# Sigmoid attention followed by a gated feed-forward layer: group 0's keys taken by key tiles, one query load and one sigmoid moved

## The chip, the cores and the metric

The kernel runs on one core of one Trainium2 chip. The metric is the device time of one execution in microseconds; lower is better. Of several timed runs the median counts. Beside the timed runs one execution was profiled, and every view below is of that execution.

The engines are called as in the profile: PE is the matrix engine (PEld its weight loads), DVE the vector engine, ACT the scalar engine, POOL and SP two engines that do little here but issue transfers. POOL's transfers convert fp32 in memory to fp16 on chip; SP's don't convert.

## The reference

Inputs are `q`, `k`, `v` of shape (8, 12, 448, 64), `w_in` (768, 2048), `w_out` (2048, 768) and `beta` (2048). The output has 8 x 448 = 3584 rows of 768.

```python
scores = q @ k.T / sqrt(64) - log(448)          # per batch and head, 448 x 448
attn   = 1 / (1 + exp(-scores))                 # a sigmoid, no sum over keys
x      = (attn @ v), heads side by side         # (3584, 768)
h      = x @ w_in
g      = h * 1 / (1 + exp(-beta * h))
out    = g @ w_out
```

## The kernel before

**Groups.** A group is four heads of one batch, laid on 128 partitions as four strips of 32, so a batch has three groups (0, 1, 2) and there are 24 in all. A strip's 32 partitions hold 14 consecutive rows each; in the code a partition's 14 rows are its "blocks" `c`. The 448 keys are worked in four key tiles: three of 128 and a last one of 64. Key tile j takes, of every partition, the rows j, j + 3, j + 6 and j + 9; the last tile takes rows 12 and 13. So the columns that belong to one key tile lie in four pieces in a partition's row.

**One group's way.** `load_one` (L110) brings a group's queries or keys as fp16 into `raw`. `transpose` turns them on DVE: queries by L191, the first three key tiles in one instruction by L199, the last by L203. Scores are matmuls of the transposed keys and queries (L213) into PSUM tiles `sco`, each of two banks. ACT turns a whole `sco` tile into attention weights (L224). `attend` multiplies them with the values (L279), and DVE copies the result as fp16 to `xT` (L288). `load_v` (L131, L138) loads a batch's values.

**The layer behind it.** `dense1` is one unit of work: six matmuls (L166) of `xT` with 128 columns of `w_in` into one PSUM bank, a sigmoid on ACT with `beta` as scale (L305), and a product on DVE (L308) into `gt`. `dense2` and, for most rows, a seven-product scheme multiply `gt` with `w_out`; stores go out from SP. There are four single PSUM banks for these units and the attention results, handed out in turn; a unit waits for the DVE instruction that last read its bank.

**Order.** All instructions are ordered by hand. The units stand in one list, and `fill_units(n)` emits the next n of them between pieces of attention. Batch 0 is special: it is done in two halves of 224 queries. `half_visit(g, c0, second)` makes the scores of half a group, for key tiles 0 and 1 (`second` = 0) or 2 and 3, and `attend` follows. The first halves of all three groups come first, with a few idle matmuls between them (L533), then the second half of group 0, then `dense1` units 0 to 15 for the first half (unit `dc` uses columns 128 dc on), between which stand the second halves of groups 1 and 2. From batch 1 on, `visit(g, jt)` makes the scores of all queries and one key tile, and a planner with fixed costs (`M1H_US` and others) decides how many units follow each visit. A visit emits its score matmuls, then two attention sigmoids, then the units.

**Loads at the start.** Group 0's first query half and all its keys come as fp32 through SP's queue (L517) into memory that `gt` uses later. DVE and ACT cast them to fp16: queries on DVE (L537), the first half of each partition's key columns on DVE (L540), the second half on ACT (L539). Everything else comes through POOL's queue, in this order: queries' first half and keys of groups 1 and 2, values of batch 0, the second query halves of groups 0, 1 and 2, then `w_in` in eight chunks of 256 columns (`load_w_in`, L148), so that chunk c feeds units 2c and 2c + 1, then group 3, `w_out` (L156) and the values of batch 1. POOL's queue works in order. The program gives its transfers eight semaphores in turn, and a transfer waits for the landing of the eighth before it.

Of the kernel before, what the change touches and what calls it, by code (L numbers as in the profile page):

```python
# [8 lines left out]
FP32 = mybir.dt.float32  # L9
FP16 = mybir.dt.float16  # L10
# [3 lines left out]
def kernel(  # L14
# [10 lines left out]
    nc = tc.nc  # L25
# [3 lines left out]
    B, H, S, D = q.shape  # L29
    NTOK, DM = out.shape  # L30
    DFF = moe_w_in.shape[1]
    P = 128
    BLK = 32
# [152 lines left out]
    def transpose(g: int, r: int, c0: int = 0, c1: int = NB):  # L186
        raw = raws[g][:, r]
        if r == 0:
            if g not in qT:
                qT[g] = qTp.tile([P, NB * BLK, PAIR], FP16, tag="qT", name="qT")  # L190
            nc.vector.transpose(  # L191
                out=in_order(g // QPB, qT[g][:, c0 * BLK : c1 * BLK]),
                in_=raw[:, c0:c1].rearrange("p c d -> p (c d)").bitcast(FP32),
            )
            return
        kT[g] = kTp.tile([P, S, PAIR], FP16, tag="kT", name="kT")
        to = kT[g].rearrange("p k e -> p (k e)").bitcast(FP32)
        frm = raw.rearrange("p c d -> p (c d)").bitcast(FP32).rearrange("p (c f) -> p c f", c=NB)
        nc.vector.transpose(  # L199
            out=to[:, 0 : JF * P].rearrange("p (j i q) -> p i j q", j=JF, i=HQ),  # L200
            in_=frm[:, 0:NF].rearrange("p (i j) f -> p i j f", j=JF),
        )
        nc.vector.transpose(  # L203
            out=to[:, JF * P :], in_=frm[:, NF:].rearrange("p c f -> p (c f)")
        )

    def score_tile():
# [23 lines left out]
        return at  # L231


    def visit(g: int, jt: int, also=()):
        if jt < JF:
            todo = [(score_tile(), [s]) for s in (2 * g, 2 * g + 1)]
        else:
            todo = [(score_tile(), [2 * h, 2 * h + 1]) for h in (g, *also)]
        for e in range(PAIR):
            for sco, slots in todo:  # L240
                for s in slots:
                    for hh in range(2):
                        score(sco, 0, s, jt, hh, e, 0, S)
        for sco, slots in todo:
            at = weigh(sco, S)
            for s in slots:
                at_tiles[s, jt, 0] = at
# [259 lines left out]
    with tc.manual_schedule():  # L507
        raws[0] = rawp.tile([P, 2, NB, D], FP16, tag="raw", name="raw")
        wide = gt.rearrange("p a b -> p (a b)").bitcast(FP32)
        cut = NH * D  # L510
        early = [(0, 0, NH), (1, 0, NB)]
        staged = {}
        at = 0
        for r, c0, c1 in early:
            staged[r] = wide[:, at : at + (c1 - c0) * D]
            at += (c1 - c0) * D
            nc.sync.dma_start(  # L517
                out=staged[r],
                in_=(q, k)[r][0, 0:HQ].rearrange("h (p c) d -> (h p) (c d)", c=NB)[
                    :, c0 * D : c1 * D  # L520
                ],
            )
        nc.gpsimd.memset(dummy, 0.0)  # L523
        nc.scalar.activation(out=dummy, in_=dummy, func=AF.Sigmoid, bias=0.0, scale=1.0)

# [7 lines left out]
                nc.tensor.matmul(idle, still[:, 0:P], still, start=True, stop=True)  # L533

        idle_units(9)
        raw = raws[0].rearrange("p r c d -> p r (c d)")
        nc.vector.tensor_copy(out=raw[:, 0, 0:cut], in_=staged[0])  # L537
        transpose(0, 0, 0, NH)
        nc.scalar.copy(out=raw[:, 1, cut:], in_=staged[1][:, cut:])  # L539
        nc.vector.tensor_copy(out=raw[:, 1, 0:cut], in_=staged[1][:, 0:cut])  # L540
        transpose(0, 1)
        for g in range(1, QPB):
            load_one(g, 0, 0, NH)
            load_one(g, 1)
        load_v(0)
        nc.sync.dma_start(out=beta_in[0:NDC], in_=moe_beta.rearrange("(c p) -> c p", p=P))
        for g in range(QPB):
            load_one(g, 0, NH, NB)
        for c in range(WCH):
            load_w_in(c)  # L550
        for g in range(1, QPB):
            transpose(g, 0, 0, NH)
# [10 lines left out]
        half_visit(0, QH, 0)  # L563
        attend(1, 0, QH)
        half_visit(0, QH, 1)
        for g in range(1, QPB):
            transpose(g, 0, NH, NB)
        attend(2, 0, QH, (0,))
        attend(2, 0, QH, (1,))
# [12 lines left out]
        firsts.close()  # L582
        share_psum(ctx, 2, 4)
        fill_units(4)
        for g in range(1, QPB):
            for second in range(2):
                half_visit(g, QH, second)
                if second:
                    attend(g - 1, QH, QH)
                fill_units(g if second else 2 + g)  # L590
        fill_units(1)
        attend(QPB - 1, QH, QH)
        fill_units(1)
        transpose(QPB, 0)
        transpose(QPB, 1)
# [24 lines left out]
        for i, (g, jt, also) in enumerate(visits):  # L620
            if jt == 0:
# [68 lines left out]
```

## Time and profile before

| what | value |
|---|---|
| timed runs | 383.72, 383.92, 384.61 us; median 383.92 |
| profiled execution | 383.76 us, of which the span of instructions is 382.0 |
| PE busy | 375.9 us, 98% of the span |
| DVE, ACT, POOL busy | 231.8, 229.5, 66.4 us |
| granted PE clock | 1.00 |
| transfers | 34.71 MB in 42405 packets |

The page cuts the span in 40 equal slices of 9.55 us and gives the busy share of each engine in tenths. The chain of waits follows the last instruction back to what released it, step by step. A timeline's row has the start, the length, the engine, the line, what is written and read, and in brackets the idle time just before and what ended it. Matmuls are pipelined and their ends are modelled, so a pause of PE is read more safely from starts than from ends. The GB/s of the transfer views count bytes written on chip; where POOL's queue converts, twice as many are read.

### The profile page before, as it was taken

How to read it: one execution, taken by the hardware profiler on the slowest of the kernel's cores; microseconds unless marked ns; L12 is line 12 of the kernel's file. 1: busy time of each engine (PE TensorE's matmuls, PEld its weight loads, DVE VectorE, ACT ScalarE, POOL GpSimd, SP SyncE). 2: the span in 40 equal slices, each digit the busy share in tenths (PEclk: the TensorE clock that was granted, in tenths of full speed). 3: DMA queues.
4: the chain of work that ended last, by engine and by line, in shares of the span. 5: the costliest groups of instructions: out<-in, count | busy, mean ns of one | idle time of the engine just before them, and what ended most of it. 6: DMA issues, size and time to landing. Idle time of an engine off the chain costs nothing.

```text
span 382.0 us, 8227 instructions
## 1 busy us (share of the span) xinstructions
PE 375.9 (98%) x3415; PEld 199.2 (52%) x3415; DVE 231.8 (61%) x439; ACT 229.5 (60%) x330; POOL 66.4 (17%) x114
## 2 busy tenths in 40 slices
PE   8999999999999999999999999999999999999996
PEld 3478754444654445444554445544456444555563
DVE  3447366775765557555775657665676665655761
ACT  5987856697465786487355782477752787435200
POOL 7833343140110410040110410113100000000000
PEclk9999999999999999999999999999999999999999
DMA  9999999845363930563363750649303300030033
GB/s 165 172 196 204 198 205 209 178 65 59 50 132 83 122 51 2 130 90 32 50 132 84 102 69 2 131 88 118 50 0 84 85 1 2 2 82 0 2 82 125
DMA packets 42405, 34.71 MB, mean 91 GB/s; under 512 B 21872, under 2 KB 38656, under 8 KB 42368
## 3 DMA queue, kind: packets, MB, share of 16 engines
q0 software_dynamic: 36688, 22.47, 43.5%
q1 hardware_dynamic: 5680, 11.71, 11.6%
q8 instruction: 27, 0.44, 0.5%
q14 instruction: 10, 0.08, 0.1%
HBM read 45.62 MB, written 11.01 MB: 148 GB/s over the span
## 4 chain that ended last, share of the span: by engine, by line
PE 92%; DMA 4%; POOL 1%; issue 1%; ACT 0%; DVE 0%; ACTq 0%; POOLq 0%
PE m_ps L166 73%; PE sco L213 10%; PE av_ps L279 9%; DMA w_in<-in_moe_w_in_dram 3%; DMA raw<-in_k_dram 2%; POOL raw L110 1%; POOL w_in L148 1%; ACT attnT L224 0%; ACT sg L305 0%; DVE osb L340 0%; DVE gt L308 0%; POOL dummy L523 0%; ACTq L305 0%; POOLq L674 0%
## 5 line engine op out<-in xcount | busy, mean ns | idle before, releaser
L224 ACT ACTIVATE attnT<-sco 128x896 f16<-128x896 f32 (+1 forms) x171 | 145.2, 902 | 81.1 <-PE sco L213 80.5
L166 PE MATMUL m_ps<-xT,w_in 128*128 128x448 f16 (+2 forms) x1014 | 154.7, 336 | 0.7 <-DMA w_in<-in_moe_w_in_dram 0.5
L308 DVE TENSOR_TENSOR gt<-m_ps,sg 128x448 f16<-128x448 f32 (+1 forms) x144 | 81.4, 572 | 81.6 <-ACT sg L305 78.1
L166 PEld LDWEIGHTS <-w_in 128*128 128x128 f16 (+1 forms) x1014 | 82.8, 101 | 69.3 <-issue 15.1
L305 ACT ACTIVATE sg<-m_ps,beta_sb 128x448 f32<-128x448 f32 (+1 forms) x144 | 84.3, 597 | 36.9 <-PE m_ps L166 29.8
L166 PEld LDWEIGHTS <-sum 128*64 128x64 f16 (+1 forms) x664 | 48.1, 104 | 33.5 <-issue 7.9
L213 PE MATMUL sco<-qT,kT 32*128 32x448 f16 (+3 forms) x864 | 52.0, 341 | 0.7 <-DVE kT L199 0.5
L166 PE MATMUL m_ps<-w_T,sum 128*128 128x384 f16 (+1 forms) x360 | 51.6, 327 | 0.0
L110 POOL DMA_DIRECT2D raw<-in_q_dram x26 | 14.4, 553 | 181.0 <-DVE kT L203 175.5
L428 DVE TENSOR_TENSOR osb<-m_ps,osb 128x384 f32<-128x384 f32 x60 | 33.3, 555 | 18.8 <-PE m_ps L166 16.9
L166 PEld LDWEIGHTS <-gt 128*128 128x128 f16 (+1 forms) x414 | 31.4, 103 | 23.8 <-issue 6.2
L279 PE MATMUL av_ps<-attnT,v 128*64 128x448 f16 (+3 forms) x432 | 40.2, 338 | 0.0
L398 DVE TENSOR_TENSOR sum<-gt 128x1024 f16<-128x1024 f16 x60 | 39.1, 677 | 0.1
L288 DVE CAST xT<-av_ps 128x448 f16<-128x448 f32 (+1 forms) x54 | 28.5, 567 | 15.3 <-PE av_ps L279 14.3
L166 PE MATMUL m_ps<-w_T,gt 128*64 128x384 f16 (+1 forms) x268 | 34.3, 327 | 0.0
L166 PE MATMUL m_ps<-w_out,sum 128*64 128x384 f16 (+1 forms) x304 | 33.8, 327 | 0.0
L279 PEld LDWEIGHTS <-v 128*64 128x64 f16 (+1 forms) x432 | 20.6, 108 | 18.8 <-issue 9.2
L213 PEld LDWEIGHTS <-kT 32*128 32x128 f16 (+1 forms) x864 | 13.7, 96 | 28.6 <-issue 25.7
L166 PE MATMUL m_ps<-w_out,gt 128*128 128x384 f16 (+3 forms) x146 | 22.6, 327 | 0.0
L131 POOL DMA_DIRECT2D v<-in_v_dram x32 | 19.8, 632 | 10.4 <-DMA w_in<-in_moe_w_in_dram 5.6
L191 DVE STREAM_TRANSPOSE qT<-raw 128x448 f32<-128x448 f32 (+1 forms) x27 | 16.6, 616 | 0.4 <-DMA raw<-in_q_dram 0.3
L431 ACT COPY osb<-m_ps 128x384 f32<-128x384 f32 x12 | 5.8, 481 | 16.8 <-PE m_ps L166 16.8
(25 smaller groups left out, 90.1 us busy)
## 6 DMA issues: line engine op xcount, KB each, us to landing
out_dram<-osb SPq DMA_DIRECT2D x98, 96.0 KB, 1.9
raw<-in_k_dram POOLq DMA_DIRECT2D x23, 224.0 KB, 5.3
raw<-in_q_dram POOLq DMA_DIRECT2D x21, 224.0 KB, 3.9
v<-in_v_dram POOLq DMA_DIRECT2D x32, 144.0 KB, 6.5
w_in<-in_moe_w_in_dram POOLq DMA_DIRECT2D x8, 384.0 KB, 10.7
w_out<-in_moe_w_out_dram POOLq DMA_DIRECT2D x4, 768.0 KB, 13.8
v<-in_v_dram POOLq DMA_DIRECT2D x16, 48.0 KB, 5.9
out_dram<-osb SPq DMA_DIRECT2D x2, 384.0 KB, 3.0
```

Source lines behind the costliest of these rows:

```text
L110: nc.gpsimd.dma_start(out=raws[g][:, r, c0:c1].rearrange("p c d -> p (c d)"), in_=(q, k)[r][b, HQ * t : HQ * (t + 1)].rearrange("h (p c) d ...
L131: nc.gpsimd.dma_start(out=vs[b][i * BLK : (i + 1) * BLK, :, 0:JF].rearrange("p h j d -> p h (j d)"), in_=rows[:, :, JF * i * D : JF * (i + ...
L166: nc.tensor.matmul(to[c : c + step], hidden[:, c : c + step], weights, **({} if step == P else {"tile_position": (0, c)}), **flags,)
L191: nc.vector.transpose(out=in_order(g // QPB, qT[g][:, c0 * BLK : c1 * BLK]), in_=raw[:, c0:c1].rearrange("p c d -> p (c d)").bitcast(FP32),)
L213: nc.tensor.matmul(sco[base : base + nk, hh, u0 : u0 + n], kT[g][lo : lo + BLK, jt * P : jt * P + nk, e], qT[g][lo : lo + BLK, c0 : c0 + n ...
L224: nc.scalar.activation(out=at[:, :, 0:n], in_=sco[:, :, 0:n], func=AF.Sigmoid, bias=NEG_LOG_S, scale=MSCALE,)
L279: nc.tensor.matmul(av[hh * D : (hh + 1) * D, 0:n], vs[b][base : base + nk, 2 * (s % NPAIR) + hh, jt], at[base : base + nk, hh, 0:n], start ...
L288: nc.vector.tensor_copy(out=xTs[b][:, s % NPAIR, c0 : c0 + n], in_=av[:, 0:n])
L305: nc.scalar.activation(out=sg[:, 0:n], in_=m1[:, 0:n], func=AF.Sigmoid, bias=0.0, scale=beta_sb[:, dc : dc + 1])
L308: nc.vector.tensor_tensor(out=gt[:, dc, off : off + n], in0=m1[:, 0:n], in1=sg[:, 0:n], op=ALU.mult)
L398: nc.vector.tensor_tensor(out=sums[t, i], in0=x, in1=y, op=op)
L428: nc.vector.tensor_tensor(out=out, in0=in0, in1=in1, op=op)
```

## The change

Three things are changed. PE's instructions stay the same in number and order.

1. Group 0's keys come in three transfers instead of one, cut by key tiles: tiles 0 and 1, tile 2, the last tile. The queries' transfer stays ahead of them. The runs of consecutive bytes are shorter: 512 runs of 512 bytes, 512 of 256, 128 of 512, where there were 128 of 3584. The casts are cut the same way: tile 0 on DVE, tile 1 on ACT, tile 2 and the last on DVE. A new function `transpose_keys(g, j0, j1)` transposes a range of key tiles, and for group 0 it is called for tiles 0 and 1, then (after the casts of the others) for tile 2 and for the last.
2. Group 2's second query half is loaded after four chunks of `w_in` instead of ahead of all eight, and its transpose moves from before `attend(2, 0, ...)` to before `attend(0, QH, QH)`. The loop over the second halves is written out; the units between them are the same.
3. In the third visit of batch 1 (index 2 of the list of visits) one `dense1` unit is emitted between the two attention sigmoids, and the planner counts it. On PE its place is the same; on ACT its sigmoid now stands between the two others.

```diff
-        kT[g] = kTp.tile([P, S, PAIR], FP16, tag="kT", name="kT")
+        transpose_keys(g, 0, JF)
+        transpose_keys(g, JF, JF + 1)
+
+    def transpose_keys(g: int, j0: int, j1: int):
+        if g not in kT:
+            kT[g] = kTp.tile([P, S, PAIR], FP16, tag="kT", name="kT")
         to = kT[g].rearrange("p k e -> p (k e)").bitcast(FP32)
-        frm = raw.rearrange("p c d -> p (c d)").bitcast(FP32).rearrange("p (c f) -> p c f", c=NB)
+        frm = raws[g][:, 1].rearrange("p c d -> p (c d)").bitcast(FP32)
+        frm = frm.rearrange("p (c f) -> p c f", c=NB)
+        if j0 == JF:
+            nc.vector.transpose(
+                out=to[:, JF * P :], in_=frm[:, NF:].rearrange("p c f -> p (c f)")
+            )
+            return
         nc.vector.transpose(
-            out=to[:, 0 : JF * P].rearrange("p (j i q) -> p i j q", j=JF, i=HQ),
-            in_=frm[:, 0:NF].rearrange("p (i j) f -> p i j f", j=JF),
-        )
-        nc.vector.transpose(
-            out=to[:, JF * P :], in_=frm[:, NF:].rearrange("p c f -> p (c f)")
+            out=to[:, j0 * P : j1 * P].rearrange("p (j i q) -> p i j q", i=HQ, q=BLK),
+            in_=frm[:, 0:NF].rearrange("p (i j) f -> p i j f", j=JF)[:, :, j0:j1],
         )
...
-    def visit(g: int, jt: int, also=()):
+    def visit(g: int, jt: int, also=(), between=None):
...
-        for sco, slots in todo:
+        for x, (sco, slots) in enumerate(todo):
+            if x and between:
+                between()
             at = weigh(sco, S)
...
-        for r, c0, c1 in early:
-            staged[r] = wide[:, at : at + (c1 - c0) * D]
...
+        k0 = wide[:, 0 : NB * D].rearrange("p (c d) -> p c d", c=NB)
+        q0 = wide[:, NB * D : (NB + NH) * D].rearrange("p (c d) -> p c d", c=NH)
...
+        def by_tile(t, j0: int, j1: int):
+            return t[:, 0:NF].rearrange("p (i j) d -> p i (j d)", j=JF)[:, :, j0 * D : j1 * D]
+
+        nc.sync.dma_start(out=q0, in_=q0_in[:, 0:NH])
+        nc.sync.dma_start(out=by_tile(k0, 0, 2), in_=by_tile(k0_in, 0, 2))
+        nc.sync.dma_start(out=by_tile(k0, 2, JF), in_=by_tile(k0_in, 2, JF))
+        nc.sync.dma_start(out=k0[:, NF:], in_=k0_in[:, NF:])
...
-        nc.vector.tensor_copy(out=raw[:, 0, 0:cut], in_=staged[0])
+        nc.vector.tensor_copy(out=raw_q[:, 0:NH], in_=q0)
         transpose(0, 0, 0, NH)
-        nc.scalar.copy(out=raw[:, 1, cut:], in_=staged[1][:, cut:])
-        nc.vector.tensor_copy(out=raw[:, 1, 0:cut], in_=staged[1][:, 0:cut])
-        transpose(0, 1)
+        nc.scalar.copy(out=by_tile(raw_k, 1, 2), in_=by_tile(k0, 1, 2))
+        nc.vector.tensor_copy(out=by_tile(raw_k, 0, 1), in_=by_tile(k0, 0, 1))
+        transpose_keys(0, 0, 2)
+        nc.vector.tensor_copy(out=by_tile(raw_k, 2, JF), in_=by_tile(k0, 2, JF))
+        nc.vector.tensor_copy(out=raw_k[:, NF:], in_=k0[:, NF:])
+        transpose_keys(0, 2, JF)
+        transpose_keys(0, JF, JF + 1)
...
-        for g in range(QPB):
+        for g in range(QPB - 1):
             load_one(g, 0, NH, NB)
         for c in range(WCH):
+            if c == WCH // 2:
+                load_one(QPB - 1, 0, NH, NB)
             load_w_in(c)
...
-        for g in range(1, QPB):
+        for g in range(1, QPB - 1):
             transpose(g, 0, NH, NB)
         attend(2, 0, QH, (0,))
         attend(2, 0, QH, (1,))
...
-        for g in range(1, QPB):
-            for second in range(2):
-                half_visit(g, QH, second)
-                if second:
-                    attend(g - 1, QH, QH)
-                fill_units(g if second else 2 + g)
-        fill_units(1)
-        attend(QPB - 1, QH, QH)
+        half_visit(1, QH, 0)
+        fill_units(3)
+        half_visit(1, QH, 1)
+        transpose(2, 0, NH, NB)
+        attend(0, QH, QH)
+        fill_units(1)
+        half_visit(2, QH, 0)
+        fill_units(4)
+        half_visit(2, QH, 1)
+        attend(1, QH, QH)
+        fill_units(3)
+        attend(2, QH, QH)
         fill_units(1)
...
-            visit(g, jt, also)
+            visit(g, jt, also, (lambda: fill_units(1)) if i == 2 else None)
...
             budget += spread[i] if i < len(spread) else rest
+            if i == 2:
+                spent += M1H_US
```

More of the change, by code (lines that the diff above doesn't have):

```diff
@@ L509 @@
         wide = gt.rearrange("p a b -> p (a b)").bitcast(FP32)
[L510 to L513, printed above, removed]
-        for r, c0, c1 in early:
-            staged[r] = wide[:, at : at + (c1 - c0) * D]
[L516 to L522, printed above, removed]
+        k0 = wide[:, 0 : NB * D].rearrange("p (c d) -> p c d", c=NB)
+        q0 = wide[:, NB * D : (NB + NH) * D].rearrange("p (c d) -> p c d", c=NH)
+        k0_in = k[0, 0:HQ].rearrange("h (p c) d -> (h p) c d", c=NB)
+        q0_in = q[0, 0:HQ].rearrange("h (p c) d -> (h p) c d", c=NB)
+        def by_tile(t, j0: int, j1: int):
[4 more added lines that the diff above has]
+        nc.sync.dma_start(out=k0[:, NF:], in_=k0_in[:, NF:])
         nc.gpsimd.memset(dummy, 0.0)
@@ L535 @@
         idle_units(9)
-        raw = raws[0].rearrange("p r c d -> p r (c d)")
-        nc.vector.tensor_copy(out=raw[:, 0, 0:cut], in_=staged[0])
+        raw_q, raw_k = raws[0][:, 0], raws[0][:, 1]
+        nc.vector.tensor_copy(out=raw_q[:, 0:NH], in_=q0)
         transpose(0, 0, 0, NH)
-        nc.scalar.copy(out=raw[:, 1, cut:], in_=staged[1][:, cut:])
-        nc.vector.tensor_copy(out=raw[:, 1, 0:cut], in_=staged[1][:, 0:cut])
-        transpose(0, 1)
+        nc.scalar.copy(out=by_tile(raw_k, 1, 2), in_=by_tile(k0, 1, 2))
[5 more added lines that the diff above has]
+        transpose_keys(0, JF, JF + 1)
         for g in range(1, QPB):
```

## The prediction

> **What bounds the kernel now.** I read the page first, then the chain of waits between 20 and 50 us, then the timelines of PE, POOL and DVE in the first 36 us, and last the DMA view by stretches.
>
> From the page: TensorE is busy 98% of the span, the sixteen DMA engines are full for about the first 70 us only, and the chain that ended last is PE nearly everywhere.
>
> ```profile
> span 382.0 us, 8227 instructions
> PE 375.9 (98%) x3415; PEld 199.2 (52%) x3415; DVE 231.8 (61%) x439; ACT 229.5 (60%) x330; POOL 66.4 (17%) x114
> ...
> DMA  9999999845363930563363750649303300030033
> ...
> PE 92%; DMA 4%; POOL 1%; issue 1%; ACT 0%; DVE 0%; ACTq 0%; POOLq 0%
> ```
>
> So only what starts PE earlier or closes a hole in PE can show in the time, and the holes are few. The chain between 20 and 50 us (start, length, what) has the two that this change aims at: PE waits for a chunk of `w_in` until 24.01, and for a multiply on VectorE (L308), itself behind a late sigmoid, until 47.54.
>
> ```profile
> 14.00 9.96 DMA w_in<-in_moe_w_in_dram
> 23.96 0.05 issue
> 24.01 0.75 PE m_ps L166 x6
> ...
> 46.61 0.46 ACT sg L305
> 47.07 0.02 issue
> 47.09 0.40 DVE gt L308
> ...
> 47.54 1.31 PE m_ps L166 x12
> ```
>
> The third hole is the start. The timeline of DVE shows when group 0's keys are there, and PE's first scores start at 5.75, after 0.54 of idleness that ends with L199:
>
> ```profile
> 4.52 0.47 DVE L540 CAST raw<-gt 128x448 f16<-128x448 f32 x1 [0.25 <-DMA gt<-in_k_dram]
> 5.12 0.58 DVE L199 STREAM_TRANSPOSE kT<-raw 128x384 f32<-128x384 f32 x1
> 5.62 0.20 DVE L203 STREAM_TRANSPOSE kT<-raw 128x64 f32<-128x64 f32 x1
> ```
>
> The view that decides most is POOL's timeline. Eight of its transfers are in flight, and each new one waits for the landing of the eighth before it, so its waits tell when the chunks of `w_in` land. Chunk 3 landed at 23.96 by the chain and POOL went on at 24.25, 0.29 later; the same 0.29 taken off the other rows gives chunk 4 at 26.30, 5 at 28.36, 6 at 30.35 and 7 at 32.29.
>
> ```profile
> 24.25 0.88 POOL L156 DMA_DIRECT2D w_out<-in_moe_w_out_dram  x1 [1.14 <-DMA w_in<-in_moe_w_in_dram]
> 26.59 0.62 POOL L131 DMA_DIRECT2D v<-in_v_dram  x1 [1.46 <-DMA w_in<-in_moe_w_in_dram]
> 28.65 0.61 POOL L131 DMA_DIRECT2D v<-in_v_dram  x1 [1.44 <-DMA w_in<-in_moe_w_in_dram]
> 30.64 0.61 POOL L131 DMA_DIRECT2D v<-in_v_dram  x1 [1.37 <-DMA w_in<-in_moe_w_in_dram]
> 32.58 0.61 POOL L131 DMA_DIRECT2D v<-in_v_dram  x1 [1.33 <-DMA w_in<-in_moe_w_in_dram]
> ```
>
> PE's timeline tells when it wants them. A `dense1` unit is six matmuls (L166) and chunk c feeds units 2c and 2c + 1, counted from 0; the four at 19.19 are units 0 to 3:
>
> ```profile
> 22.16 1.32 PE L166 MATMUL m_ps<-xT,w_in 128*128 128x224 f16 x12
> 24.01 0.75 PE L166 MATMUL m_ps<-xT,w_in 128*128 128x224 f16 x6 [0.52 <-DMA w_in<-in_moe_w_in_dram]
> ...
> 27.43 2.47 PE L166 MATMUL m_ps<-xT,w_in 128*128 128x224 f16 x24
> 29.84 0.70 PE L213 MATMUL sco<-qT,kT 32*128 32x224 f16 x16
> ...
> 31.38 1.90 PE L166 MATMUL m_ps<-xT,w_in 128*128 128x224 f16 x18
> ```
>
> Four units and a change to scores take 27.43 to 29.84, 2.41; five (34.13 to 37.11, same view) take 2.98; so a unit is 0.57. Unit 6 could start at 22.16 + 2 x 0.57 = 23.30 and starts at 24.01: that hole is 0.7, not the 0.52 in brackets, which counts from a modelled end. Unit 8 (chunk 4) wants its weights at 27.43, 1.1 after they landed. Unit 10 (chunk 5) wants them at 28.57, only 0.21 after. Unit 12 (chunk 6) has 1.0, and unit 14 (chunk 7), at 31.38 + 1.14 = 32.52, has 0.23. PE resumes 0.05 after a landing, so 0.16 and 0.18 are what it can gain before chunk 5 or 7 stops it.
>
> **The change, part by part.** The sum is made against the profiled execution, 383.76 (span 382.0 and 1.8 around it), which lies 0.16 under the median 383.92 of the three timed runs. The instructions on PE stay the same in number and order.
>
> *The sigmoid.* Four units from 44.89 would let the fifth start at 44.89 + 4 x 0.57 = 47.17; it starts at 47.54, so the hole is 0.37 by starts. The cause is on ScalarE: two attention sigmoids (45.00, 1.73 together) run ahead of the first `dense1` sigmoid (46.61), so its bank comes free at 47.49. Moved between them, that sigmoid starts at 45.8 and ends at 46.3, L308 (0.39) ends by 46.7, and the fifth unit doesn't wait. The second attention sigmoid now ends at about 47.1, the second `dense1` sigmoid at 47.4, its L308 at 47.8, so the sixth unit, due at 47.74, waits about 0.1. Gain 0.27, between 0.1 and 0.37.
>
> *Group 2's second query half moved past four chunks.* Each chunk is 768 packets; the half is 112 KB, and the DMA view of 13 to 14 us, when such halves pass, moves 183 GB/s, so 0.6 for it. Chunks 0 to 3 land about 0.6 sooner and chunk 3 at about 23.4, which takes the 0.7 hole away or leaves 0.1 of it. Chunks 4 to 7 have the same bytes ahead of them as before and land when they did. So of 0.7 only 0.16 survives at unit 10: the wait moves from chunk 3 to chunk 5. On POOL no issue waits longer in a way that matters: group 3's queries now wait for chunk 1 instead of 0, 2 us later, with 13 us of queue still ahead of them. On DVE the transpose of that half (0.37 to 0.40, L191) leaves the stretch at 18 us and now stands ahead of the casts L288 at 26.34; DVE is idle there for 0.68, and the half lands near 24.5, so nothing queued behind it waits. It is wanted by scores at 26.92.
>
> *Keys by tiles.* The one key DMA (128 runs of 3584 bytes) becomes three (512 runs of 512, 512 of 256, 128 of 512): 8 packets on each of 16 engines become 32 + 32 + 8. In the DMA view of 3 to 4 us the hardware queue has 98 packets of 3584 bytes (and 11 marks) in 88% of 16 engine-us: 143 ns each. The last store, 128 packets of 1024 bytes (379.5 to 381 us), takes 24.7% of 24 engine-us: 46 ns each. A line through both gives 27 ns for 512 bytes and 17 for 256, an estimate below its last point. First piece: 32 x 27 = 0.86 instead of 8 x 143 = 1.14 for all keys, so it lands near 4.25 rather than 4.5. Then the ScalarE cast of 256 instead of 448 columns (0.56 down to about 0.4) and the transpose, between 0.41 (224 columns) and 0.58 (384), 0.43: 4.25 + 0.4 + 0.43 + 0.1 = 5.2. PE's idle matmuls end at 5.2 as well. The first scores come 0.5 earlier; ends 0 and 0.6. DVE gains four instructions (two more casts, 0.2 to 0.39 each by the row of 0.39, one more transpose), all before group 1's queries land at about 6.1 and the keys at 8.0, and the second scores want tile 2 by 7.0 only. From there ScalarE's sigmoids run end to end (12 from 6.65 to 16.1) and carry the lead to PE's 19.19.
>
> All three pieces together are 32 x 27 + 32 x 17 + 8 x 27 = 1.62 us of each engine's time against 1.14: 0.5 more ahead of POOL's queue. That queue doesn't fill the engines at first: 151 GB/s over 4 to 8 us against 196 over 19 to 31, 0.9 us of slack. So the queue behind is late by between 0 and 0.5; I take 0.25, the middle, since nothing shows how well the two queues fill each other's gaps. [...]
>
> *Sum.* Sigmoid -0.27. Weights: chunk 5 lets PE go 0.16 earlier if it lands as before, and lands 0.25 later, so +0.09; the lead of 0.5 and the hole of 0.7 both end there. Together -0.18: 383.58 for an execution like the profiled one, 383.7 as a median of runs.
>
> **Rivals.** *The weights come sooner (faster).* POOL's queue has weak stretches: 155 GB/s from 16 to 19 us against 196 after, 3 x (1 - 155/196) = 0.63 lost, and 0.9 from 4 to 8. If the new order loses 0.5 less there, chunk 5 is no bound until PE is 0.16 + 0.5 ahead: 383.76 - 0.27 - 0.66 = 382.8; with everything taken (0.5 + 0.7 + 0.27) 382.3. For it: nothing in the profile says that the loss belongs to the place in time. Against: bytes and order after chunk 3 are the same.
>
> *Short runs are dear (slower).* If each short run cost what a 1792-byte packet of the queries does, 75 ns by the line above, 72 of them take 5.4 instead of 1.14; less the slack of 0.9 the queue is 3.4 late, and PE with it at chunks 3 to 7: 383.76 - 0.27 - 0.16 + 3.4 = 386.7. It decides from 1.3 of lateness, about (1.14 + 0.9 + 1.3) / 72 = 46 ns a packet. Against: 1024-byte packets already take no more than 46. For: no row shows this queue with more than 128 runs in a transfer.
>
> *The head doesn't move.* The first piece lands no earlier than the whole key did, or group 1's keys (8.0, transposed by 8.6) hold the second group's scores, due at 9.22 - 0.5. Then the lead is 0 to 0.3, and since chunk 5 caps it anyway, the time is the forecast's, 383.6 to 383.9.
>
> **How the numbers follow.** Forecast 0.44, head without lead 0.20, weights sooner 0.22, short runs dear 0.14. A measurement of this kernel tells about 0.2% (0.77 us) from no change, so faster is below 383.15 and slower above 384.69. The first two cases lie between: same 0.64; faster 0.22; slower 0.14. The range takes most of the faster case, 382.8, and reaches with the full 0.5 of lateness and the spread of the runs (384.61 at most before) to 384.6; about 2 in 10 lie outside.
>
> **What would show it.** In the profile after: first scores near 5.2; no PE wait at unit 6 (near 23) and one for `w_in` of 0.3 to 0.8 at unit 10 or 14; POOL's rows that follow chunks 4 to 7 within 0.4 of the old ones; no wait for L308 at 47 over 0.15. I am wrong if chunk 5 lands before 28.0 or after 29.5, if the first scores start after 5.75, or if a new wait stands on the path after 50 us.

## The result, and the profile after

The change makes the kernel slower. Its median is 386.25 us (384.71 to 387.99, 12 runs) against 383.88 (383.07 to 384.92, 12 runs) before: ratio 1.0062, 95% interval 1.0046 to 1.0077. Forecast were 383.7 and a range up to 384.6.

The profiled execution of the change is its quickest, 384.71 us, with the PE clock granted at 1.000. In 10 of the other 11 runs the granted clock was 0.990 to 0.996. So this profile holds about 0.9 us of the loss, and a second profile of the same kernel (the last experiment, 385.55 us, clock 0.996) has to show the rest. The eleventh of the others, 387.16 us, stood at 1.000 as well and has no profile; what made it long stays open.

The page of the change, its span, engines and chain:

```profile
span 382.9 us, 8234 instructions
PE 375.2 (98%) x3415; PEld 199.1 (52%) x3415; DVE 232.1 (61%) x442; ACT 229.0 (60%) x330; POOL 66.4 (17%) x114
...
PE 96%; DMA 2%; DVE 0%; ACT 0%; SPq 0%; issue 0%; DVEq 0%
PE m_ps L166 74%; PE sco L221 12%; PE av_ps L289 9%; DMA gt<-in_k_dram 2%; PE idle_ps L542 1%; ACT attnT L232 0%; DVE osb L350 0%; SPq L529 0%; SPq L528 0%; DVE raw L551 0%; DVE kT L210 0%; DVE raw L552 0%; DVEq L551 0%
```

The DMA that the chain goes through was `w_in` and is now `gt<-in_k_dram`, group 0's own keys: 2% of the span, 7.1 us. PE is 0.7 us less busy over a span 0.9 us longer, so this execution lost time by waiting, not by slower work. DVE's timeline names the piece:

```profile
5.07 0.43 DVE L549 CAST raw<-gt 128x256 f16<-128x256 f32 x1 [0.71 <-DMA gt<-in_k_dram]
5.61 0.45 DVE L210 STREAM_TRANSPOSE kT<-raw 128x256 f32<-128x256 f32 x1
8.85 0.29 DVE L551 CAST raw<-gt 128x256 f16<-128x256 f32 x1 [2.79 <-DMA gt<-in_k_dram]
9.06 0.22 DVE L552 CAST raw<-gt 128x128 f16<-128x128 f32 x1
9.19 0.30 DVE L210 STREAM_TRANSPOSE kT<-raw 128x128 f32<-128x128 f32 x1
```

L549 and L551 are the casts of tiles 0 and 2. Tile 2's transfer, issued by SP at 1.64, landed at 8.76 by the chain, 7.1 us later; before, all keys were there for the cast at 4.52. The chain's piece:

```profile
1.64 7.11 DMA gt<-in_k_dram
```

PE's timeline shows what hangs on it, and that the two holes further on are gone; first before, then after:

```profile
5.75 0.86 PE L213 MATMUL sco<-qT,kT 32*128 32x224 f16 x16 [0.54 <-DVE kT L199]
...
7.52 0.80 PE L213 MATMUL sco<-qT,kT 32*128 32x224 f16 x16
...
44.89 2.47 PE L166 MATMUL m_ps<-xT,w_in 128*128 128x224 f16 x24
...
48.78 0.59 PE L213 MATMUL sco<-qT,kT 32*64 32x448 f16 x8
```

```profile
6.12 0.58 PE L221 MATMUL sco<-qT,kT 32*128 32x224 f16 x16 [1.12 <-DVE kT L210]
6.63 1.04 PE L542 MATMUL idle_ps<-still 128*128 128x512 f16 x4
9.55 0.70 PE L221 MATMUL sco<-qT,kT 32*128 32x224 f16 x16 [1.89 <-DVE kT L210]
...
24.10 1.90 PE L166 MATMUL m_ps<-xT,w_in 128*128 128x224 f16 x18
...
46.20 3.72 PE L166 MATMUL m_ps<-xT,w_in 128*128 128x224 f16 x36
49.85 0.39 PE L221 MATMUL sco<-qT,kT 32*64 32x448 f16 x4
```

The second scores start at 9.55 instead of 7.52. Units 4 to 6 run as one group from 24.10, with no wait for chunk 3. The six units at 46.20 run as one, 3.65 to the next scores, where they took 44.89 to 48.78 = 3.89 before. POOL's rows that follow chunks 3, 4 and 5 (0.29 taken off: landings at 24.06, 26.69 and 28.66; before 23.96, 26.30 and 28.36) moved by 0.1 to 0.4:

```profile
24.35 1.78 POOL L156 DMA_DIRECT2D w_out<-in_moe_w_out_dram  x2 [1.42 <-DMA w_in<-in_moe_w_in_dram]
26.98 0.62 POOL L131 DMA_DIRECT2D v<-in_v_dram  x1 [0.85 <-DMA w_in<-in_moe_w_in_dram]
28.95 0.62 POOL L131 DMA_DIRECT2D v<-in_v_dram  x1 [1.36 <-DMA w_in<-in_moe_w_in_dram]
```

How the lateness runs through, all starts from PE's timelines and differences to the profile of before (unit 8 stands behind the old hole for chunk 3, the last group behind the moved sigmoid). The rows below the first are experiments:

| profile | time | second scores (7.52) | unit 0 (19.19) | unit 8 (27.43) | last group (373.15) | span (382.0) |
|---|---|---|---|---|---|---|
| the change | 384.71 | +2.03 | +1.93 | +1.31 | +1.08 | +0.9 |
| the change, second profile | 385.55 | +1.49 | +2.77 | +2.15 | +1.93 | +1.8 |
| keys by tiles alone | 386.85 | +2.52 | +3.83 | +3.21 | +3.23 | +3.1 |
| 14 idle matmuls | 384.92 | +2.10 | +2.00 | +1.38 | +1.15 | +1.0 |
| one key transfer | 382.95 | +0.06 | -0.04 | -0.67 | -0.88 | -0.9 |

The first row is lost in the second scores (2.0) and gets back 0.62 at the old chunk 3 hole and 0.24 at the moved sigmoid. The third row, where the load isn't moved, gets back the same 0.62: PE comes to unit 6 so late that chunk 3 is there anyhow. So the 0.62 doesn't show a gain from the move. The second row loses another 1.28 between the second scores and unit 0.

### The profile page after: what moved, and what is told of

It is laid out like the page before. It is cut to its first block, busy times and chain, and to the rows that moved or that the text cites. A ratio compares the mean times of both kernels' runs of the same rounds, so it can differ in the third digit from the quotient of the medians.

```text
span 382.9 us, 8234 instructions
## 1 busy us (share of the span) xinstructions
PE 375.2 (98%) x3415; PEld 199.1 (52%) x3415; DVE 232.1 (61%) x442; ACT 229.0 (60%) x330; POOL 66.4 (17%) x114
## 4 chain that ended last, share of the span: by engine, by line
PE 96%; DMA 2%; DVE 0%; ACT 0%; SPq 0%; issue 0%; DVEq 0%
PE m_ps L166 74%; PE sco L221 12%; PE av_ps L289 9%; DMA gt<-in_k_dram 2%; PE idle_ps L542 1%; ACT attnT L232 0%; DVE osb L350 0%; SPq L529 0%; SPq L528 0%; DVE raw L551 0%; DVE kT L210 0%; DVE raw L552 0%; DVEq L551 0%
```

## The experiments

The theory at the start: the key pieces behind the first meet POOL's loads in the DMA engines and land about 4 us late; PE waits, and the wait costs clock as well. Its rivals: the other two parts do the harm; short packets are dear by themselves; or it is the number of SP's packets beside POOL's that counts, whatever their bytes, which the expectations call the theory of turns. Edits are against the changed kernel unless told otherwise.

**Part 1 alone.** The other two parts are undone:

```diff
-        for g in range(QPB - 1):
+        for g in range(QPB):
             load_one(g, 0, NH, NB)
         for c in range(WCH):
-            if c == WCH // 2:
-                load_one(QPB - 1, 0, NH, NB)
             load_w_in(c)
...
-            visit(g, jt, also, (lambda: fill_units(1)) if i == 2 else None)
+            visit(g, jt, also)
...
```

> Only the first part of the change (group 0's keys loaded, cast and transposed by key tiles); the load order of group 2 and the sigmoid are as before. [...] Then tile 2 lands between 6 and 9 us, PE waits for the second scores until about 9.5 as in the profile after, the wait for chunk 3 near 24 is gone because PE is late, and the time is as much above before as the whole change or 0.3 more: +2.4 to +2.9 us, 386.3 to 386.8. Rival, the moved load of group 2 does the harm: then this kernel is within 0.5 us of before.

Measured: 387.29 us (386.59 to 389.19, 4 runs) against 383.85; ratio 1.0100, 1.0068 to 1.0132. The harm is all in part 1, and more than all: half a microsecond over the range that was expected. PE's timeline and its view by windows of 3.41 us (length, then busy time and count of PE, PEld, DVE, ACT and POOL, then granted clock, DMA share, GB/s):

```profile
10.04 0.70 PE L221 MATMUL sco<-qT,kT 32*128 32x224 f16 x16 [3.21 <-DVE kT L210]
```

```profile
4.82:8.23 3.41, 1.80 (x21) 0.63 (x20) 0.41 (x1) 1.73 (x2) 1.88 (x4) 1.00 1.06 165
8.23:11.64 3.41, 1.60 (x20) 0.57 (x20) 2.39 (x9) 0.84 (x2) 1.96 (x4) 1.00 1.52 186
11.64:15.05 3.41, 3.41 (x33) 1.29 (x36) 0.61 (x3) 2.23 (x4) 2.55 (x4) 0.50 1.34 152
```

The wait grew to 3.21, and one window behind it ran at half clock: 1.31 us more between the second scores and unit 0 (+2.52 to +3.83 in the table).

**Parts 2 and 3 alone.** Group 0's keys are loaded, cast and transposed in the old way:

```diff
-        nc.sync.dma_start(out=by_tile(k0, 0, 2), in_=by_tile(k0_in, 0, 2))
-        nc.sync.dma_start(out=by_tile(k0, 2, JF), in_=by_tile(k0_in, 2, JF))
-        nc.sync.dma_start(out=k0[:, NF:], in_=k0_in[:, NF:])
+        early = [(0, 0, NH), (1, 0, NB)]
...
-        transpose_keys(0, 0, 2)
...
-        transpose_keys(0, 2, JF)
-        transpose_keys(0, JF, JF + 1)
+        transpose(0, 1)
```

> The change without its first part: keys of group 0 in one transfer as before, group 2's second half behind four chunks, sigmoid moved. Theory of turns and my cap by chunk 5: hole of 0.7 us at unit 6 gone, a wait of 0.2 to 0.6 us for chunk 5 or 7 in its place, no wait for L318 (the product on DVE) near 47; 0.3 to 0.5 us faster than before, 383.4 to 383.6. Rival, the moved load does the harm: +1 us or more. Rival, weights come sooner: no wait for w_in at all and 0.9 to 1.1 us faster, 382.8 to 383.0.

Measured: 383.78 (382.79 to 384.80, 12 runs) against 383.85; ratio 0.9994, 0.9979 to 1.0009. In the profile the waits for chunk 3 and for the late sigmoid are gone, and the wait expected at chunk 5 or 7 didn't come. But its head had a hole of 0.65 before the first scores and matmuls at half speed until 10.3 (four idle matmuls at 6.73 take 1.89, not 1.04), so it was 1.61 late at unit 0, which alone would take away the wait for chunk 3, and ends at a span of 382.8. No gain shows in the median; the interval still allows one of 0.8.

**More idle matmuls in the wait.** To take only the clock's part away:

```diff
-                    idle_units(4 if g < QPB - 1 else 2)
+                    idle_units(14 if (g, second) == (0, 0) else 4 if g < QPB - 1 else 2)
```

> The changed kernel with 14 instead of 4 idle matmuls between group 0's first and second scores, 2.4 us more of PE work where PE waits for tile 2. Theory of the cold clock: in most runs of the changed kernel the granted clock is 0.990 to 0.996 and the span up to 3 us over the profiled one, because PE stands idle 2 us or more before its second scores; with idle work the clock stays at 1.000 and the median falls from 386.25 to 384.7 to 385.3. Rival, the runs differ because tile 2 itself lands 1 to 4 us later in them: the median stays at 386 to 386.5, whatever the clock.

Measured: 384.97 (384.58 to 387.35, 10 runs); ratio 1.0035, 1.0018 to 1.0052; granted clock 0.999 or 1.000 in nine of the ten. Tile 2 is as late as ever, but PE is kept busy until 8.9 (timeline):

```profile
5.69 3.19 PE L542 MATMUL idle_ps<-still 128*128 128x512 f16 x14
9.62 0.70 PE L221 MATMUL sco<-qT,kT 32*128 32x224 f16 x16 [0.74 <-DVE kT L210]
10.25 1.04 PE L542 MATMUL idle_ps<-still 128*128 128x512 f16 x4
```

So of the loss of 2.4 us about 1.3 is the clock (386.25 - 384.97; by the interval of this run, 0.7 to 2.0 us of loss are left, so 0.4 to 1.7), and the other 1.1 is the wait less the 0.62 and 0.24 that PE gets back later.

**One transfer, still cast by tiles.** The three key transfers become one with long runs; all else of the change stays:

```diff
-        nc.sync.dma_start(out=by_tile(k0, 0, 2), in_=by_tile(k0_in, 0, 2))
-        nc.sync.dma_start(out=by_tile(k0, 2, JF), in_=by_tile(k0_in, 2, JF))
-        nc.sync.dma_start(out=k0[:, NF:], in_=k0_in[:, NF:])
+        nc.sync.dma_start(
+            out=k0.rearrange("p c d -> p (c d)"), in_=k0_in.rearrange("p c d -> p (c d)")
+        )
```

> The changed kernel with group 0's keys in one transfer of 128 long runs again, but cast and transposed by tiles as in the change. Theory of turns: keys land at 4.5 us as before, first scores start at about 5.55 instead of 5.75 and the second scores don't wait; behind it as the kernel without the first part, 0.3 to 0.6 us faster than before (383.3 to 383.6), the lead of 0.2 being taken by chunk 5. Rival, the order of casts and transposes on DVE does the harm: second scores wait past 8.5 here too, and the time is 1 us or more over before.

Measured: 382.98 (382.52 to 386.06, 12 runs); ratio 0.9985, 0.9967 to 1.0003. PE's timeline:

```profile
7.58 0.70 PE L221 MATMUL sco<-qT,kT 32*128 32x224 f16 x16
...
22.12 1.90 PE L166 MATMUL m_ps<-xT,w_in 128*128 128x224 f16 x18
...
26.76 2.47 PE L166 MATMUL m_ps<-xT,w_in 128*128 128x224 f16 x24
```

No wait is left at the second scores, at chunk 3 or at chunk 5, and the span is 381.1. The whole loss hangs on the keys' transfers, not on the cut casts and transposes.

**POOL held until the keys are there**, to see the short runs without company:

```diff
+        hold = const.tile([P, 2], FP32, name="hold")
+        nc.gpsimd.tensor_copy(out=hold[:, 0:1], in_=k0[:, 2, 0:1])
+        nc.gpsimd.tensor_copy(out=hold[:, 1:2], in_=k0[:, NF, 0:1])
         for g in range(1, QPB):
             load_one(g, 0, 0, NH)
             load_one(g, 1)
```

> The changed kernel, but POOL first copies one column of tile 2's and of the last tile's staged keys, so that none of its loads starts before group 0's keys have landed. Same three key transfers with the same short runs on SP's queue. Theory of turns: with nobody to take turns with, tile 2 lands before 5.3 us (8.76 in the profile after) and the last tile before 5.5. Rival, short runs are dear in themselves (each run slow, or SP's queue slow to make so many): tile 2 lands after 6 here too. The whole is slower all the same, by 2 to 5 us against before, since everything else starts 3 to 4 us later.

Measured: 389.01 us (one execution), since everything of POOL's comes late; the question is the keys. DVE's timeline, and the queues from 4 to 9 us (packets, MB, share of 16 engines' time), first of this run, then of the change:

```profile
4.43 0.29 DVE L549 CAST raw<-gt 128x256 f16<-128x256 f32 x1 [0.22 <-DMA gt<-in_k_dram]
...
5.34 0.30 DVE L551 CAST raw<-gt 128x256 f16<-128x256 f32 x1
5.56 0.21 DVE L552 CAST raw<-gt 128x128 f16<-128x128 f32 x1
```

```profile
q0 software_dynamic: 271, 0.33, 46.4%
q1 hardware_dynamic: 544, 0.16, 13.3%
```

```profile
q0 software_dynamic: 627, 0.66, 87.6%
q1 hardware_dynamic: 712, 0.21, 20.2%
```

Alone, tile 2 needs no wait on DVE at all (landed 5.08, and the last tile 5.26), with the same packets. A packet of SP's queue took 13.3% x 80 us / 544 = 20 ns alone and 20.2% x 80 / 712 = 23 ns beside POOL's loads. By size the trace has 18 ns for 256 bytes and 27 for 512 alone. Short packets are not dear here, and they are hardly dearer in company; they wait between packets. By the trace's packet records the 512 packets of 256 bytes start between 3.36 and 4.70 alone, and in the change, where each takes 21 ns, between 4.09 and 8.23, while POOL's take 88% of the engines' time.

**All keys twice.** If the number of SP's packets set the landing, few long ones would land sooner. Tile 2 and the last tile come from a second transfer of all the keys, 8 packets of 3584 bytes for each engine in place of 40 short ones:

```diff
-        nc.sync.dma_start(out=by_tile(k0, 2, JF), in_=by_tile(k0_in, 2, JF))
-        nc.sync.dma_start(out=k0[:, NF:], in_=k0_in[:, NF:])
+        at = (NB + NH) * D
+        k1 = wide[:, at : at + NB * D].rearrange("p (c d) -> p c d", c=NB)
+        nc.sync.dma_start(
+            out=k1.rearrange("p c d -> p (c d)"), in_=k0_in.rearrange("p c d -> p (c d)")
+        )
...
```

> The changed kernel with tile 2 and the last tile taken out of a second transfer of all keys in 128 long runs: 448 KB instead of 224 KB, but 8 packets per engine instead of 40. Theory of turns: 8 turns with POOL's packets instead of 40, so it lands near 6 (5.5 to 6.6) in spite of twice the bytes; second scores wait 0 to 0.5 us instead of 1.9, no half-clock window behind them, and the time is 383.0 to 384.3. Rival, the bytes or the load on the engines make tile 2 late: it lands at 8.8 or later, and the time is 386 or more.

Measured: 386.83 (386.49 to 387.76, 8 runs); ratio 1.0075, 1.0050 to 1.0099. DVE's timeline:

```profile
9.13 0.29 DVE L554 CAST raw<-gt 128x256 f16<-128x256 f32 x1 [3.95 <-DMA gt<-in_k_dram]
```

The second transfer landed at 9.04, as late as 40 short packets with half the bytes. So the number of packets alone doesn't set it, and the theory that gave 5.5 to 6.6 fell. Bytes were doubled along with it, so the run can't tell how far each counts. In this profile two windows in a row ran at half clock (9.19 to 16.01).

**POOL's first loads from memory already read.** Another way to account for it: first reads make POOL's packets slow, and SP's wait behind them.

```diff
...
-            load_one(g, 0, 0, NH)
-            load_one(g, 1)
+            load_one(g, 0, 0, NH, src=0)
+            load_one(g, 1, src=0)
```

> The change whole, but POOL's first loads (groups 1 and 2, first query half and all keys) read group 0's memory again, so their outputs are made from other numbers; queues, sizes and order are as in the change. Theory A, the first reads of fresh memory make POOL's packets slow and SP's tile 2 waits behind slow packets: tile 2 lands by 6.5 to 7 us instead of 8.76, the second scores start by 7.8. Theory B, SP's later pieces share the engines with POOL's loads whatever is read: tile 2 lands between 8 and 9.2, the second scores start between 9 and 10, after 1.5 to 3 us of idle PE.

Measured: 387.29 (one execution), clock 0.991; the cast of tile 2 on DVE:

```profile
8.75 0.29 DVE L551 CAST raw<-gt 128x256 f16<-128x256 f32 x1 [3.58 <-DMA gt<-in_k_dram]
```

Theory A fell: tile 2 was as late with POOL reading memory that had been read before.

**Group 2's loads held.** Only group 1's two POOL loads stay beside SP's pieces:

```diff
+        hold = const.tile([P, 2], FP32, name="hold")
         for g in range(1, QPB):
+            if g == 2:
+                nc.gpsimd.tensor_copy(out=hold[:, 0:1], in_=k0[:, 2, 0:1])
+                nc.gpsimd.tensor_copy(out=hold[:, 1:2], in_=k0[:, NF, 0:1])
             load_one(g, 0, 0, NH)
```

> The change whole, but POOL issues group 2's loads and all behind them only once group 0's tile 2 and last tile are there; group 1's two loads still run beside SP's pieces. If SP's later pieces end when the POOL loads that lie beside them are through, with only group 1's two in the way they land by 6 to 6.8 us and the second scores wait 0.5 us at most. If a single POOL load beside them is enough to hold them off, they land at 8 or later as in the change (8.76), and the second scores wait 1.5 us or more.

Measured: 390.27 us (one execution; the later loads are late, as in the run with POOL held). DVE's timeline:

```profile
7.36 0.29 DVE L551 CAST raw<-gt 128x256 f16<-128x256 f32 x1 [2.18 <-DMA gt<-in_k_dram]
7.58 0.22 DVE L552 CAST raw<-gt 128x128 f16<-128x128 f32 x1
```

Between the two expectations: tile 2 landed at 7.27, the last tile at 7.44, and PE waited 1.29. By the trace's landing marks POOL's second load was through at 7.06. With all of POOL's loads five profiles have tile 2 between 6.93 and 9.10 and the last tile between 8.48 and 9.52. So the last of SP's pieces lands at 5.3 with no POOL load beside it, at 7.4 with two, at 8.5 to 9.5 with all of them: the more of POOL's loads are queued, the later. Tile 2 by itself doesn't show that order: one of the five, 6.93, is below the 7.27 with two.

**One idle matmul more in the kernel before.** The head of before has its own hole, 0.54, and its runs spread over 1.85 us. The theory, which the expectations call the cold start: the hole decides whether full speed comes early or late (the trace's first full-speed clock record stands at 6.42 in the profile of before and at 10.28 in that of parts 2 and 3 alone), and a tenth idle matmul (edit against before) takes the spread away.

```diff
-        idle_units(9)
+        idle_units(10)
```

> The kernel before with 10 instead of 9 idle matmuls at the start, 0.43 us more at half clock, which fills most of the hole of 0.54 before the first scores. Theory of the cold start: in a part of the runs of before (8 of 29 at 384.7 to 385.2) and of the kernel without the first part, the hole makes PE miss a window of 3.41 us, so that the clock is granted one window later; with the hole under 0.2 these runs vanish: highest of the undisturbed runs under 384.5, median 383.3 to 383.6. Rival, that spread comes from the landing of the weights: median and spread as before, 383.85, or up to 0.2 more.

Measured: 383.63 (382.85 to 384.94, 12 runs) against 383.53; ratio 0.9991, 0.9970 to 1.0012. The spread stayed at 2.1 us, so this is not confirmed. (By the record 7 of the 29 earlier runs lie at 384.7 or more, not 8.) The run showed something else: chunk 3 had landed by 23.04 (POOL's timeline, 0.29 off) and the hole at unit 6 was not there, with the old order of loads.

```profile
23.33 0.88 POOL L156 DMA_DIRECT2D w_out<-in_moe_w_out_dram  x1 [1.08 <-DMA w_in<-in_moe_w_in_dram]
```

**One transfer and ten idle matmuls, with and without the moved load.** The kernel with one key transfer takes `idle_units(10)`; the second of the pair also loads group 2's second query half at its old place.

> The kernel with one key transfer, casts and transposes by tiles, moved load and moved sigmoid, and 10 instead of 9 idle matmuls at the start: the hole of 0.32 before the first scores is filled. Theory of the cold start: median 382.7 to 383.0 with fewer runs over 383.5 than the 3 of 12 before. Rival: no difference, or 0.1 to 0.2 us slower because the tenth idle matmul ends after the keys are there.

> One long-run key transfer with the casts and transposes by tile, the moved sigmoid and ten idle units, without the move of group 2's second query half. If that move is worth its hole (0.7 us for chunk 3 before), PE waits 0.5 to 0.9 us for w_in near 23 us here, and the time is 0.2 to 0.7 us above the same kernel with the move (383.17). If the weights land early enough anyhow, or the cap by chunk 5 gives the gain back, the two are within 0.2 us.

Measured: with the move 383.17 (382.38 to 384.12, 12 runs) against 383.53, ratio 0.9975, 0.9955 to 0.9995; without it 383.21 (382.78 to 385.18, 12 runs) against 384.65, ratio 0.9977, 0.9960 to 0.9994. Both intervals lie just below 1, so both are a little faster than the kernel before, and they lie well below the change; between them no difference can be told. The median of 382.7 to 383.0 that the theory of the cold start gave was not reached; over 383.5 lie 1 run of 12 with the move and 3 of 12 without it, where the kernel with nine idle matmuls had 3. With the move PE's timeline still has a wait for chunk 3:

```profile
23.39 0.75 PE L166 MATMUL m_ps<-xT,w_in 128*128 128x224 f16 x6 [0.24 <-DMA w_in<-in_moe_w_in_dram]
```

The profile without the move is its slowest run, 385.18, and PE and POOL show why:

```profile
25.67 0.75 PE L166 MATMUL m_ps<-xT,w_in 128*128 128x224 f16 x6 [2.06 <-DMA w_in<-in_moe_w_in_dram]
```

```profile
25.91 0.88 POOL L156 DMA_DIRECT2D w_out<-in_moe_w_out_dram  x1 [2.62 <-DMA w_in<-in_moe_w_in_dram]
```

Chunk 3 landed at 25.62 there. The row that tells it is POOL's second load of `w_out`; in the profile of part 1 alone, where the load isn't moved either, it is this one:

```profile
25.55 0.88 POOL L156 DMA_DIRECT2D w_out<-in_moe_w_out_dram  x1 [1.16 <-DMA w_in<-in_moe_w_in_dram]
```

Over ten profiles, by this row less 0.29 (with the load moved, the first of the two joined rows), chunk 3 landed at 23.96, 25.26, 23.04 and 25.62 with the old order, and at 24.06, 23.19, 22.83, 23.40, 22.50 and 23.33 with the load moved. The landing differs by up to 2.6 us between profiles with the same order. The averages, 24.5 and 23.2, agree with a gain from the move, which by its bytes is worth some 0.6 (an estimate: 112 KB at the 183 GB/s of 13 to 14 us before), but the two ranges overlap.

**The change once more.** The same kernel, for a profile nearer its median.

> The change itself once more, for a profile that is nearer to its median than the one at 384.71 us. If the later key pieces' lateness and the clock after it are the cause, a profile between 385.5 and 387.5 us shows the second scores between 9 and 10 us after an idle stretch of 1.5 to 3.3 us, and one or two windows of 3.4 us at half clock right behind it (granted clock 0.991 to 0.996); no wait for w_in near 24 us and none for gt near 47 us. If the cause lay later in the kernel, the head would be as in the profile at 384.71 us with a clock of 1.000 and some other row would hold the 1 to 2 us.

Measured: 386.78 (385.55 to 387.60, 6 runs); ratio 1.0073, 1.0047 to 1.0100. The profile, 385.55, shows what the first one lacks. PE's timeline, and PE's windows with the granted clock (third column from the end):

```profile
5.25 0.89 PE L221 MATMUL sco<-qT,kT 32*128 32x224 f16 x16
6.07 1.04 PE L542 MATMUL idle_ps<-still 128*128 128x512 f16 x4
9.01 0.87 PE L221 MATMUL sco<-qT,kT 32*128 32x224 f16 x16 [1.90 <-DVE kT L210]
9.81 1.89 PE L542 MATMUL idle_ps<-still 128*128 128x512 f16 x4
```

```profile
5.98:9.39 3.41, 1.51 (x24) 0.51 (x20) 1.18 (x6) 1.73 (x2) 1.52 (x4) 1.00 1.25 188
9.39:12.80 3.41, 3.41 (x29) 1.09 (x30) 1.52 (x6) 1.55 (x3) 2.83 (x5) 0.50 1.66 184
12.80:16.21 3.41, 3.41 (x42) 1.30 (x40) 0.92 (x2) 3.24 (x5) 3.41 (x5) 1.00 1.28 159
```

The first scores are early (5.25). Here the last tile is the late one: its cast ran at 8.50, tile 2's at 7.02. Behind the wait the clock is 0.50 from 9.39 to 12.80, exactly 3.41 us, and the four idle matmuls take 1.89 in place of 1.04. By the table: +1.49 from the wait, +1.28 from the clock, -0.62 and -0.24 given back, and the span is 1.8 longer. The last tile is also the later of the two in the other four profiles with cut transfers and all of POOL's loads.

Two pauses of the same length, 1.89 and 1.90 us, so cost nothing in the one profile and a window at half clock in the other. The first profile has no half clock in its head, so nothing in it shows where a window would begin. Laid from the trace's first clock record, at 4.65, which is the author's guess, two windows of 3.41 us split the pause (7.6 to 9.55) between them:

```profile
4.65:8.06 3.41, 1.89 (x22) 0.63 (x20) 0.87 (x2) 1.74 (x3) 1.96 (x4) 1.00 1.06 170
8.06:11.47 3.41, 1.92 (x30) 0.87 (x34) 2.53 (x10) 1.56 (x3) 2.02 (x4) 1.00 1.45 188
```

In the second profile the whole pause lies in the 3.41 us ahead of the fall, 5.98 to 9.39, which hold 1.51 us of PE work. Laid from 6.00 to 9.41, the first profile's stretch would hold 1.55, so it is the laying that tells the two apart.

## Why the prediction was wrong

**The step that failed** is the overlap of the two queues in "Keys by tiles". The prediction has DVE's new instructions run "all before group 1's queries land at about 6.1", and "the second scores want tile 2 by 7.0 only". The deadline is right. The landing that this takes for granted is the packets' own time: the first piece at 4.25, then 32 x 17 and 8 x 27 ns, so about 5.0 for the last. With POOL held that sum holds: the pieces landed at 4.40, 5.08 and 5.26, with packets of 18 and 27 ns. But the only queue that the prediction makes late by their meeting is POOL's ("I take 0.25"; its rows moved by 0.1 to 0.4, which agrees). What SP's own later pieces lose beside the loads that POOL issues from 1.3 us on was put at nothing, without a reason. Before the change the same meeting cost nothing on the path: all keys stood in one transfer, issued at 1.2 and landed by 4.5, and what met POOL's loads was `beta`. Cutting it put 2 of 3 pieces among POOL's first loads. Measured over five profiles, the last piece lands at 8.5 to 9.5, and PE waits 1.9 to 3.2 us where nothing fills the pause.

**A price that was missing**: the clock. A wait on PE was counted at its length only, but in 10 of the first 12 runs of the change, and in all 6 later ones, the granted clock was below 0.997. It is so in only 3 of the 82 runs of the kernel before that the experiments took, and in 1 of 12 with one key transfer. One window of 3.41 us at half speed cost 1.3 (profiles with a mean clock of 0.996); two in a row, as in the profiles at 0.990 and 0.991, cost 2.4 and 2.2 between the second scores and unit 0 (all keys twice, and POOL reading group 0's memory). The half clock lasts 3.41 us in the change again (9.39 to 12.80) and in part 1 alone (11.64 to 15.05), and twice that with all keys twice (9.19 to 16.01). PE wasn't idle ahead of it: the 3.41 us before a fall in the head hold 1.51 us of PE work (the change again), 1.60 (part 1 alone), 1.23 (all keys twice) and 1.72 (POOL reading group 0's memory). Nor does the length of the pause decide: 1.89 us of it cost no clock in the first profile and 1.90 cost a window in the second. How the pause lies in windows of 3.41 us would fit: in the heads of these profiles those with 1.72 us of PE work or less were followed by half clock, those with 1.80 or more (part 1 alone from 4.82, both of the first profile) were not. But for the first profile this rests on the guess that its windows run from 4.65, which no run shows. And it isn't the whole rule, since with POOL held a later window of 1.97 us of work (17.24 to 20.65) was followed by half clock too.

**The other terms.** The lead of the head, "first scores 5.2", came in four of five profiles with cut transfers that keep POOL's loads (5.25, 5.28, 5.18, 5.23) and not in the one at 384.71, 6.12, past the 5.75 that the prediction had named as its sign of error; it was worth nothing ahead of the wait. The sigmoid: 0.27 forecast, 3.89 - 3.65 = 0.24 measured. The hole of chunk 3, 0.7, did go (0.62 in both profiles of the change), but PE's lateness alone takes it away, as part 1 alone shows. Its size is in part a draw of the execution: with the old order chunk 3 landed anywhere from 23.04, which leaves no hole, to 25.62. And the pair with and without the moved load (383.17 and 383.21) shows no gain from the move. "Chunk 5 lets PE go 0.16 earlier": with the keys in one transfer PE wanted chunk 5 at 26.76 + 1.14 = 27.90 and went through without a wait, as the chunk had landed by 27.59 (the row less 0.29) and not at 28.36, so the cap wasn't there either. It was read to a tenth of a microsecond from a landing that varies by more. A slip without effect: DVE gains three instructions, not four (439 and 442 on the pages).

**The rivals.** "Short runs are dear" had the sign, and its 386.7 is near the median, but for a reason that the runs refute: it put 75 ns on a packet, to decide from 46, and a packet took 20 to 23; it put the lateness into POOL's queue at chunks 3 to 7, and those moved by 0.1 to 0.4. A right number from it would have been luck. Before the change, too, 700 of the 713 packets from 11 to 12 us are under 512 bytes (the values' runs, in POOL's queue), and 176 GB/s were moved. "The weights come sooner" is seen in the profile with one transfer (382.95, chunk 5 by 27.59), not in the change; but with the old order and ten idle matmuls chunk 5 landed by 27.67, so the new order isn't shown to be the reason. "The head doesn't move" came true in one of the five profiles (6.12) and not in the others; it too has no term for the later pieces, so it explains none of the loss.

**What stays open.** How an engine divides its time between SP's queue and POOL's: 8 long packets an engine landed at 9.04, 40 short ones at 8.76 (tile 2) and 8.95 (the last tile), so their number alone doesn't set it, and no run shows what does. Also open are what lets the clock fall, beyond the windows above, the long run at clock 1.000, and what makes the kernel before spread over 1.9 us. One candidate, not tested: the first full-speed clock record stands at 4.65 in the first profile of the change, 6.42 in that of before and 10.28 in that of parts 2 and 3 alone.

## What to carry to other kernels

When a transfer is cut so that its first piece comes early, follow the last piece to its landing and to the instruction that waits for it, and look at which other queue begins in between: here the first scores gained 0.5 us and the last piece lost 4 to 5. A pause of 1.9 to 3.2 us on a busy PE cost another 1.3 us through its clock here, or 2.2 to 2.4, and in one profile nothing; idle matmuls in the pause took that part away in nine of ten runs. And a wait of half a microsecond for a DMA in one profile may be that execution's draw: see it in a second profile before a change is built on it.

## What the runs showed of the hardware

The later key pieces of SP's queue landed the later, the more of POOL's loads were queued beside them: the last at 5.3, 7.4 and 8.5 to 9.5 us with none, two and all of those loads, while a packet of that queue took 20 ns alone and 23 in company. Eight long packets an engine with twice the bytes came no sooner than 40 short ones. In the first profile of the change nine of tile 2's sixteen landing marks stand by 6.39 and the last at 8.76: the cast waited for the last mark and began at 8.85.

The granted clock stood at 1.00 in the first windows of the profile with parts 2 and 3 alone, while four idle matmuls at 6.73 took 1.89 us, as they do at 0.50 (1.04 at 1.00). The start at half speed doesn't appear in that column; it is read from the length of like groups, and the trace's first clock record, at 10.28, agrees.
